# Result in two column tiles of 224 and 288 with one copy each, and the softmax sums by one matmul of two columns

One Trainium2 chip, one core. The metric is device time in microseconds of one execution; medians are of all runs of a kernel.

## The reference, cut to what matters

One decode step: layer norm, attention over the last 2048 of 8192 cached positions (8 sequences, 32 query heads, 8 key/value heads of 128), output projection, then an MLP (B's token shift is zero for one token).

```python
h  = x + attention(layernorm(x)) @ wo            # softmax(q k^T / sqrt(128)) v
y  = layernorm(h)                                # B's input
x1 = y                                           # the shifted branch is zero for S == 1
h2 = gelu(layernorm(x1) @ w3) @ w4               # w3 [512,1792], w4 [1792,512]
out = h + x1 + h2                                # [8, 1, 512] bf16
```

## The kernel before

PE is the matmul engine (TensorE) and PEld its weight loads, ACT is ScalarE, DVE is VectorE, SP is SyncE, which issues nearly all loads here, 79 MB. A loop over the 8 sequences transposes K on PE, makes scores, exponentials and the product with V. PSUM is the memory that the matmuls write. After the loop comes a tail: output projection, statistics, product with w3 (L729), gelu into `gT`, product with w4 (L757), copies out of PSUM, store. Parts that the change and the argument touch (cuts marked `...`):

```python
W4_CUT = [0, 8, 12, 13, 14]        # chunks of 128 rows of w4 in each of four loads
...
def pe_LB(e):                      # softmax sums of two halves, summed in PSUM
    for half in range(2):
        ins = e.matmul(LB, lspread..., lsum[:, half:half + 1], start=(half == 0), stop=(half == 1))
    ins.then_inc(sem_LB, 1)
def dve_rL(e, b):
    e.wait_ge(sem_LB, b + 2)
    e.reciprocal(rL[:, :], LB).then_inc(dve_self, 1)
...
NQ = 4; DQ = D // NQ               # four column strips of 128
fin_ps = b6[:, 0:DQ]
def pe_fin(e):
    ...                            # the residual (hi and lo halves) into PSUM, L749
    e.wait_ge(sem_actP, ACTP_G)    # gT is there
    for fc in range(FC):           # 14 chunks of w4
        if fc in W4_CUT:
            e.wait_ge(sem_w4[W4_CUT.index(fc)], 16)
        for j in range(NQ):        # L757: strip j, written to PSUM partitions 32j..
            ins = e.matmul(fin_ps[32 * j:32 * j + B, :], gT[:, fc * B:(fc + 1) * B],
                           w4_sb[:, fc, j * DQ:(j + 1) * DQ], start=False, stop=(fc == FC - 1),
                           tile_position=(0, 32 * j), ...)
            if fc == FC - 1:
                ins.then_inc(sem_peP, 1)
def dve_final(e):                  # strips 0 and 2; act_final does 1 and 3
    for j in range(0, NQ, 2):
        e.wait_ge(sem_peP, PEP_FIN[j])
        ins = e.tensor_copy(out_sb[:, j * DQ:(j + 1) * DQ], fin_ps[32 * j:32 * j + B, :])
    ins.then_inc(sem_dveP, 1)
```

The product has 8 columns of weights, the batch (128\*8 in the profile), and the kernel sets strip j at `tile_position=(0, 32 * j)`. The strips of a chunk run beside each other: the last chunk's four matmuls, of 263 ns or more each, start from 188.74 on and are all done 0.28 us later.

## Time and profile before

| | before |
|---|---|
| time, median (range) of the first 3 runs | 193.14 us (193.06 to 193.16) |
| span of the profiled execution | 191.4 us |
| busy: PE, ACT, DVE | 76%, 49%, 45% |
| HBM read over the span | 414 GB/s (428 to 435 in most slices) |
| first w4 chunk used / last chunk used | 186.90 / 188.74 us |
| store issued | 189.72 us |

The time is that of the loads, plus a tail of 2.7 us from the last landing (188.7) to the end of the span. A change here shortens the time only if it shortens this tail, and lengthens it if it lengthens the tail or makes some engine fall behind the loads. The lines of the profile are in the prediction.

### The profile page before, as it was taken

The numbers are of one execution on the slowest core, as the hardware profiler recorded it, in microseconds if no ns is written. First come the engines' busy times: TensorE is split into PE (matmuls) and PEld (weight loads), VectorE is DVE, ScalarE is ACT, GpSimd is POOL, SyncE is SP. The second block draws the span as 40 slices with busy tenths as digits, with TensorE's granted clock in tenths as the row PEclk, the third lists the DMA queues.
The fourth block names the chain that finished last, engine by engine and source line by source line (L and its number), as shares of the span: only waits on it lengthen the run. The fifth ranks groups of instructions, "written<-read, shape, count | busy, mean of one in ns | idle before, by whom it ended". The sixth has DMA issues, their size and how long they took to land. (4 is left out here: it accounts for less than half of the span.)

```text
span 191.4 us, 6341 instructions
## 1 busy us (share of the span) xinstructions
PE 145.6 (76%) x2848; PEld 116.9 (61%) x2848; DVE 85.8 (45%) x183; ACT 94.2 (49%) x119; POOL 6.4 (3%) x17
## 2 busy tenths in 40 slices
PE   2038996499878975998589849985998599886754
PEld 0014964487676754876577639764976577676642
DVE  7922656145625560457055604571446254640031
ACT  3031772657277724671678147725672586253041
POOL 8400000000000000000000000000000000000000
PEclk9999999669999999799999987999699999999655
DMA  6999999999999999999999999999999999999991
GB/s 228 431 435 428 421 419 443 428 428 431 428 435 426 435 431 426 431 431 431 435 428 435 435 424 431 431 431 435 428 435 435 424 431 431 431 435 411 412 400 43
DMA packets 6473, 79.31 MB, mean 414 GB/s; under 512 B 688, under 2 KB 960, under 8 KB 1856
## 3 DMA queue, kind: packets, MB, share of 16 engines
q1 hardware_dynamic: 6448, 79.18, 97.3%
q8 instruction: 6, 0.10, 0.2%
q14 instruction: 3, 0.02, 0.0%
q10 hardware_dynamic: 16, 0.01, 0.0%
HBM read 79.18 MB, written 0.01 MB: 414 GB/s over the span
## 5 line engine op out<-in xcount | busy, mean ns | idle before, releaser
L436 PE MATMUL kT_ps<-perm_b,slots 128*128 128x128 bf16 x1024 | 74.4, 235 | 15.2 <-PEq L421 15.2
L458 ACT ACTIVATE kT_sb<-kT_ps 128x1024 bf16<-128x1024 bf16 x64 | 65.1, 1023 | 36.6 <-PE kT_ps L436 36.4
L436 PEld LDWEIGHTS kT_ps<-perm_b,slots 128*128 128x128 bf16 x1024 | 66.0, 106 | 25.8 <-issue 25.8
L462 DVE COPY kT_sb<-kT_ps 128x1024 bf16<-128x1024 bf16 x64 | 44.3, 692 | 65.5 <-PE kT_ps L436 65.5
L501 ACT ACTIVATE P_sb<-S_ps,mtile 128x1024 bf16<-128x1024 f32 x16 | 17.7, 1108 | 31.3 <-DVE mtile L496 31.3
L476 PE MATMUL S_ps<-kT_sb,qcur 128*32 128x512 bf16 x256 | 25.7, 392 | 0.0
L533 PE MATMUL misc<-slots,pT_sb 128*32 128x128 bf16 x1024 | 16.2, 220 | 5.9 <-PEq L421 5.9
L533 PEld LDWEIGHTS misc<-slots,pT_sb 128*32 128x32 bf16 x1024 | 14.8, 97 | 8.2 <-issue 7.7
L523 DVE TENSOR_TENSOR pT_sb<-kT_ps,mask 128x1024 bf16<-128x1024 bf16 x18 | 12.4, 691 | 7.9 <-PE kT_ps L452 7.9
L452 PE MATMUL kT_ps<-perm_p,P_sb 128*128 128x128 bf16 x144 | 11.0, 221 | 0.0
L552 PE MATMUL b<-o_sum,selw 128*128 128x32 f32 x56 | 7.4, 276 | 4.3 <-PEq L421 4.3
L452 PEld LDWEIGHTS kT_ps<-perm_p,P_sb 128*128 128x128 bf16 x144 | 8.2, 98 | 3.6 <-issue 3.6
L476 PEld LDWEIGHTS S_ps<-kT_sb,qcur 128*32 128x32 bf16 x256 | 6.6, 93 | 6.0 <-issue 0.2
L552 PEld LDWEIGHTS b<-o_sum,selw 128*128 128x128 f32 x56 | 6.8, 191 | 5.3 <-issue 5.3
L542 DVE TENSOR_SCALAR o_sum<-misc,rL 128x128 f32<-128x128 f32 x8 | 2.8, 351 | 8.1 <-PE misc L533 8.1
L286 DVE TENSOR_SCALAR ident_f<-iota_f 128x128 f32<-128x128 f32 x1 | 5.7, 5682 | 1.3 <-POOL iota_f L207 1.3
L344 PE MATMUL b<-ident_b,xln_b 8*128 8x8 bf16 x4 | 0.3, 174 | 7.5 <-DVE xln_b L320 7.5
L287 DVE TENSOR_SCALAR ident_b<-iota_f 128x128 bf16<-128x128 f32 x1 | 5.6, 5606 | 0.0
L485 DVE TENSOR_REDUCE mtile<-S_ps 128x1 f32<-128x512 f32 x8 | 5.4, 673 | 0.0
L344 PEld LDWEIGHTS b<-ident_b,xln_b 8*128 8x128 bf16 x4 | 0.2, 113 | 8.3 <-DVE xln_b L320 8.3
L664 PE MATMUL S_ps<-opl,slots 128*128 128x8 bf16 x128 | 3.7, 168 | 1.8 <-issue 1.6
L508 PE MATMUL S_ps<-lsum,lspread 128*128 128x1 f32 x36 | 5.0, 244 | 0.0
(91 smaller groups left out, 66.2 us busy)
## 6 DMA issues: line engine op xcount, KB each, us to landing
slots<-in_A_k_cache_dram SPq DMA_DIRECT2D x16, 2048.0 KB, 13.5
slots<-in_A_v_cache_dram SPq DMA_DIRECT2D x16, 2048.0 KB, 17.0
slots<-in_A_wq_dram SPq DMA_DIRECT2D x1, 4096.0 KB, 12.1
slots<-in_A_wo_dram SPq DMA_DIRECT2D x2, 1024.0 KB, 21.5
slots<-in_A_wo_dram SPq DMA_DIRECT2D x1, 2048.0 KB, 26.0
slots<-in_B_w_dram SPq DMA_DIRECT2D x2, 896.0 KB, 30.7
slots<-in_B_w_dram SPq DMA_DIRECT2D x1, 1024.0 KB, 29.4
slots<-in_B_w_dram SPq DMA_DIRECT2D x1, 512.0 KB, 28.3
```

The costliest lines, as they stand in the source:

```text
L286: e.tensor_single_scalar(ident_f[:], iota_f[:], 0.0, ALU.is_equal)
L287: ins = e.tensor_single_scalar(ident_b[:], iota_f[:], 0.0, ALU.is_equal)
L436: ins = e.matmul(kT_ps[t % 2][:, c * 128:(c + 1) * 128], src[:, c * 128:(c + 1) * 128], perm_b[:, :], is_transpose=True)
L452: ins = e.matmul(kT_ps[half][:, c * 128:(c + 1) * 128], P_sb[:, k * 128:(k + 1) * 128], perm_p[:, :], is_transpose=True)
L458: e.activation(kT_sb[:, i % NKT, 0:W // 2], kT_ps[i % 2][:, 0:W // 2], ACT.Copy).then_inc(sem_Elo, 1)
L462: e.tensor_copy(kT_sb[:, i % NKT, W // 2:W], kT_ps[i % 2][:, W // 2:W]).then_inc(sem_Ehi, 1)
L476: ins = e.matmul(S_ps[32 * gl:32 * (gl + 1), 0, :], qcur[:, GL * gq + gl, o:o + 32], kv[:, gl, :, :], start=(t == 0), stop=(t == 2 * NT - ...
L485: ins = e.tensor_reduce(mtile[:, 1, 0:1], S_ps[:, 0, :], AX.X, ALU.max)
L501: e.activation(P_sb[:, half * W // 2:(half + 1) * W // 2].rearrange("r (k g) -> r k g", g=GL), bass.AP(tensor=S_ps[:, :, :].tensor, offset ...
L523: e.tensor_tensor(bass.AP(tensor=pT_sb[:, :, :, :].tensor, offset=h0 * NT * 48, ap=[[CT * NT * 48, 128], [48, CT // 2 * NT], [32, 2], [1, ...
L533: ins = e.matmul(pv_ps[32 * q:32 * (q + 1), :], pT_sb[:, c, q, 16 * gq:16 * gq + 32], slots[:, slot, k * DH:(k + 1) * DH], start=(gq == 0 ...
L552: ins = e.matmul(op_ps(b), selw[:, q, :], o_sum[:, NJ * q:NJ * (q + 1)], start=(q == 0), stop=(q == 3))
```

## The change

Its intent: fewer and larger instructions at the end. Two strips of 224 and 288 columns give 28 matmuls in place of 56 and one copy on each of DVE and ACT in place of two; SP waits for one semaphore. The two sums of the softmax come from one two-column matmul, and DVE adds them. The diff, cut to its core:

```diff
-        NQ = 4
-        DQ = D // NQ
+        N_CUT = [0, 224, 512]
+        NQ = 2
+        DQ = D // KC
...
-        LB = S_ps[:, 1, 0:1]
+        LB = S_ps[:, 1, 0:2]
...
-                for half in range(2):
-                    ins = e.matmul(LB, lspread..., lsum[:, half:half + 1], start=(half == 0), stop=(half == 1))
-                ins.then_inc(sem_LB, 1)
+                e.matmul(LB, lspread..., lsum[:, :], start=True, stop=True).then_inc(sem_LB, 1)
...
-            e.reciprocal(rL[:, :], LB).then_inc(dve_self, 1)
+            ins = e.tensor_reduce(lhs[:, :], LB, AX.X, ALU.add)
+            chain(e, ins, "dve_self", dve_self)
+            e.reciprocal(rL[:, :], lhs[:, :]).then_inc(dve_self, 1)
...
-        fin_ps = b6[:, 0:DQ]
+        fin_at = lambda j: b6[32 * j:32 * j + B, 0:N_CUT[j + 1] - N_CUT[j]]
...                              (the residual: ten matmuls, cut at the strips' and blocks' edges)
-                    ins = e.matmul(fin_ps[32 * j:32 * j + B, :], gT[:, fc * B:(fc + 1) * B],
-                                   w4_sb[:, fc, j * DQ:(j + 1) * DQ], ...
+                    ins = e.matmul(fin_at(j), gT[:, fc * B:(fc + 1) * B],
+                                   w4_sb[:, fc, N_CUT[j]:N_CUT[j + 1]], ...
...
+        def out_tile(e, j, copy):
+            e.wait_ge(sem_peP, PEP_FIN[j])
+            copy(out_sb[:, N_CUT[j]:N_CUT[j + 1]], fin_at(j)).then_inc(sem_done, 1)
+
+        DV.append(lambda e: out_tile(e, 0, e.tensor_copy))
+        AC.append(lambda e: out_tile(e, 1, lambda o, i: e.activation(o, i, ACT.Copy)))
```

More of the change, by code (lines that the diff above doesn't have):

```diff
@@ L106, in bass_sequential_preLN__sliding_block_cached__mixer_s_mlp__decode_kernel @@
         rL = sb([128, 1], dt.float32, "rL")
+        lhs = sb([128, 1], dt.float32, "lhs")
         iota_f = sb([128, 128], dt.float32, "iota_f")
@@ L148, in bass_sequential_preLN__sliding_block_cached__mixer_s_mlp__decode_kernel @@
         sem_out = S("sem_out")
+        sem_done = S("sem_done")
         act_self = S("act_self")
@@ L267, in sp_prog @@
                                     ).then_inc(sem_w4[i], 16)
-            e.wait_ge(sem_dveP, DVEP_OUT_READY)
-            e.wait_ge(sem_actP, ACTP_OUT_READY)
+            e.wait_ge(sem_done, NQ)
             e.dma_start(out.rearrange("b s d -> (b s) d"), out_sb[:, :]).then_inc(sem_out, 16)
@@ L506, in pe_LB @@
             if e is not None:
-                for half in range(2):
-                    ins = e.matmul(LB, lspread[:, :, :].rearrange("p q h -> p (q h)"), lsum[:, half:half + 1],
-                                   start=(half == 0), stop=(half == 1))
-                ins.then_inc(sem_LB, 1)
+                e.matmul(LB, lspread[:, :, :].rearrange("p q h -> p (q h)"), lsum[:, :], start=True, stop=True).then_inc(sem_LB, 1)
         def dve_rL(e, b):
             e.wait_ge(sem_LB, b + 2)
-            e.reciprocal(rL[:, :], LB).then_inc(dve_self, 1)
+            ins = e.tensor_reduce(lhs[:, :], LB, AX.X, ALU.add)
+            chain(e, ins, "dve_self", dve_self)
+            e.reciprocal(rL[:, :], lhs[:, :]).then_inc(dve_self, 1)
             cnt["dve_self"] += 1
@@ L747, in pe_fin @@
             for half in (hpx_hi, hpx_lo):
-                for k in range(KC):
-                    e.matmul(fin_ps[32 * k:32 * k + B, :], half[:, k * B:(k + 1) * B], ident_b[:, :],
-                             start=(half is hpx_hi), stop=False, tile_position=(0, 32 * k), skip_group_check=True)
+                for j in range(NQ):
+                    for k in range(KC):
+                        n0, n1 = max(N_CUT[j], k * DQ), min(N_CUT[j + 1], (k + 1) * DQ)
+                        if n0 < n1:
+                            e.matmul(fin_at(j)[:, n0 - N_CUT[j]:n1 - N_CUT[j]], half[:, k * B:(k + 1) * B],
+                                     ident_b[:, n0 - k * DQ:n1 - k * DQ],
+                                     start=(half is hpx_hi and n0 == N_CUT[j]), stop=False,
+                                     tile_position=(0, 32 * j), skip_group_check=True)
             e.wait_ge(sem_actP, ACTP_G)
@@ L756, in pe_fin @@
                 for j in range(NQ):
-                    ins = e.matmul(fin_ps[32 * j:32 * j + B, :], gT[:, fc * B:(fc + 1) * B],
-                                   w4_sb[:, fc, j * DQ:(j + 1) * DQ], start=False, stop=(fc == FC - 1),
+                    ins = e.matmul(fin_at(j), gT[:, fc * B:(fc + 1) * B],
+                                   w4_sb[:, fc, N_CUT[j]:N_CUT[j + 1]], start=False, stop=(fc == FC - 1),
                                    tile_position=(0, 32 * j), skip_group_check=True)
@@ L762, in bass_sequential_preLN__sliding_block_cached__mixer_s_mlp__decode_kernel @@
         PE.append(pe_fin)
-        DVEP_OUT_READY = ev_dve.next()
-        def dve_final(e):
-            for j in range(0, NQ, 2):
-                e.wait_ge(sem_peP, PEP_FIN[j])
-                ins = e.tensor_copy(out_sb[:, j * DQ:(j + 1) * DQ], fin_ps[32 * j:32 * j + B, :])
-            ins.then_inc(sem_dveP, 1)
-        DV.append(dve_final)
-        ACTP_OUT_READY = ev_act.next()
-        def act_final(e):
-            for j in range(1, NQ, 2):
-                e.wait_ge(sem_peP, PEP_FIN[j])
-                ins = e.activation(out_sb[:, j * DQ:(j + 1) * DQ], fin_ps[32 * j:32 * j + B, :], ACT.Copy)
-            ins.then_inc(sem_actP, 1)
-        AC.append(act_final)
+        def out_tile(e, j, copy):
[3 more added lines that the diff above has]
+        AC.append(lambda e: out_tile(e, 1, lambda o, i: e.activation(o, i, ACT.Copy)))
         with nc.Block() as block:
```

## The prediction

> **What bounds the kernel now.** I read, in this order: the page, the chain that ended last, the DMA issues, the order in time of the last 4.6 us, and the busy time and granted clock in stretches of it. Section 2 of the page first.
>
> ```profile
> DMA  6999999999999999999999999999999999999991
> GB/s 228 431 435 428 421 419 443 428 428 431 428 435 426 435 431 426 431 431 431 435 428 435 435 424 431 431 431 435 428 435 435 424 431 431 431 435 411 412 400 43
> ...
> by line: DMA slots<-in_B_w_dram 14.8%; PE kT_ps L436 0.6%; PE b L757 0.6%; SPq L265 0.2%; ACTq L782 0.1%; ACT xln_b L778 0.1%; issue 0.1%
> ...
> 159.74 28.26 DMA slots<-in_B_w_dram
> 187.99 0.04 issue
> 188.04 1.06 PE b L757 x23
> 189.09 0.26 ACT xln_b L778
> 189.35 0.28 ACTq L782
> ```
>
> From the second slice to the last but one, the DMA engines are full (DMA digit 9) at some 430 GB/s, and 79.31 MB have to come in. No compute engine is near its limit: PE is busy 76%, ACT 49%, DVE 45%. The chain says the same: it rests on a load of w4 that lands at 187.99, and only then turns to compute: 1.06 us of the last product, two copies on ACT. What follows the landing is the one stretch where an engine's speed is the kernel's speed. This is that stretch, as the timeline gives it (start, duration, engine, line, operation, count).
>
> ```profile
> 186.87 0.77 PEld L757 LDWEIGHTS b<-slots,gT 128*8 128x8 bf16 x32 [1.05 <-ACT gT L740]
> 186.90 2.12 PE L757 MATMUL b<-slots,gT 128*8 128x128 bf16 x56 [0.80 <-DMA slots<-in_B_w_dram]
> 188.04 0.46 PEld L757 LDWEIGHTS b<-slots,gT 128*8 128x8 bf16 x20 [0.40 <-DMA slots<-in_B_w_dram]
> 188.74 0.09 PEld L757 LDWEIGHTS b<-slots,gT 128*8 128x8 bf16 x4 [0.25 <-DMA slots<-in_B_w_dram]
> 189.05 0.58 DVE L769 CAST xln_b<-b 8x128 bf16<-8x128 f32 x2 [4.29 <-PE b L757]
> 189.08 0.55 ACT L778 ACTIVATE xln_b<-b 8x128 bf16<-8x128 f32 x2 [3.00 <-PE b L757]
> 189.72 0.37 SPq L270 DMA_DIRECT2D out_dram<-xln_b  x1
> ```
>
> PE follows the loads: chunks 0 to 7 of w4 (32 weight loads, four a chunk) begin at 186.87, as the first w4 load lands; 8 to 12 at 188.04; 13 at 188.74. Between the bursts PE stands idle for w4. So PE keeps up with the loads, and after the last one there is a single chunk (0.28 us) to do. The clock matters as well; the columns are us, busy and number on PE, PEclk, DMA share, GB/s.
>
> ```profile
> 13.01 1.02 PE L367 MATMUL S_ps<-slots,xlnT 128*8 128x512 bf16 x7 [1.76 <-DMA slots<-in_A_wq_dram]
> 13.81 1.07 PE L367 MATMUL S_ps<-slots,xlnT 128*8 128x512 bf16 x8
> 14.24 1.07 PE L367 MATMUL S_ps<-slots,xlnT 128*8 128x512 bf16 x8
> 14.67 1.07 PE L367 MATMUL S_ps<-slots,xlnT 128*8 128x512 bf16 x8
> ...
> 178.38:181.79 3.41, 2.90 (x102) 0.50 1.03 420
> 181.79:185.21 3.42, 1.91 (x45) 0.50 1.01 410
> 185.21:188.62 3.41, 2.50 (x78) 0.50 0.57 217
> ```
>
> From 178.38 to the end PE is granted half of its clock. The L367 lines come from a stage of the same build (four column strips, 8 columns of weights, but 512 columns moved): its groups of four start 427 ns apart (13.81, 14.24, 14.67). Narrow windows on L757 show groups of four starting at 187.07, 187.18, 187.28, 187.40, 187.50, 187.60: 107 ns apart for 128 columns. Both are columns / 1.2 per ns for four matmuls at once. So the strips run beside each other, and a round of them costs the columns of its widest strip.
>
> [...] here a small reciprocal takes 203 ns from SBUF (L699) and 157 from PSUM (L514).
>
> **The change, part by part.**
>
> *Softmax sums.* One f32 matmul with two moving columns replaces two with one each: the trace has 4 PE entries per batch at L508, 250 ns each, started some 140 ns apart; two go, about 0.28 us of PE a batch. DVE gets a two-column reduce out of PSUM (about 0.16 to 0.21 us, from the 157 ns of the reciprocal there and the 208 ns of the small reduce L489), a wait for itself, and the reciprocal now reads SBUF (0.20 for 0.16). That is about 0.3 us more per batch. In the loop neither counts, since the DMA queue is full. In the last batch the reciprocal ends at 172.17 and its user waits for PE until 173.88: the added 0.3 us fits in the gap of 1.7. PE's 0.28 us earlier only makes the chain earlier that makes gT, and gT is ready at 186.08, 0.79 us before w4. Worth 0.
>
> *Residual into PSUM (L749).* Eight matmuls of 128 columns become ten of 32 to 128; from 185.71 at half clock, at most about 0.7 us, done before 186.87. Worth 0.
>
> *The last product (L757).* Four strips of 128 columns become two of 224 and 288. This removes half of the instructions, but also half of what runs beside each other. A chunk now takes 288 / 1.2 = 240 ns for 107. With 14 chunks: 14 x 240 = 3.36 us for 1.49. PE no longer keeps up with w4: chunk 8 could start at 186.90 + 8 x 0.24 = 188.82, after the load for it (188.0) and even the last load (188.74) have landed. So the waits for w4 disappear from the second on, and PE itself sets the end. A first matmul with 128 columns takes 263 ns, with 288 thus 263 + 160/1.2 = 396. The end of the wide strip is 186.90 + 13 x 0.24 + 0.396 = 190.42; before, it was 189.02. Cost: 1.40 us.
>
> *The copies.* Before, two per engine: 0.58 us on DVE, 0.55 on ACT. After, one each. ACT's slope is from 128 columns (269 ns, L778) to 512 (597 ns, L377): 0.854 ns a column, so 288 columns take 269 + 137 = 406 ns. DVE: 282 ns for 128, 692 for 512 (L384), so 224 columns take 385 ns, and its strip ends earlier. ACT ends at 190.42 + 0.04 + 0.41 = 190.87; before, both were done at 189.63. Gain in the copies 0.15 us. One wait of SP less is worth about 0.02 (the semaphore instruction there takes 17 ns).
>
> Sum: +1.40 - 0.15 - 0.02 = +1.23 us; the store would be issued at 190.95 for 189.72. 193.14 + 1.23 = 194.37; I take 0.05 off for the chance of a faster clock, below: 194.3.
>
> **The rivals.**
>
> *The loads still set the end.* Then only the copies' gain would stay: 193.0 us. For it speaks that the chain rests on w4. It needs a chunk in 120 ns, which is the full clock. [...] Against it: a window with PE busy 2.90 of 3.41 us (178.38 to 181.79) did not raise the clock[...]. [...] I give it one in eight.
>
> *The two strips do not overlap well.* With strictly one after the other a chunk takes (224 + 288) / 1.2 = 427 ns, 14 take 5.97 us: 2.6 us more, 196.9. The steps of L367 and L757 speak against it, as four strips overlap fully there.
>
> *The sums become a wait.* If the longer DVE path held up the next maximum and with it the loop, each batch could cost 0.3 us, 2.4 us in all. Against it: the DMA share is about 1.0 in every stretch from 15 to 185 us, so the loads have work queued throughout; and DVE waits 65.5 us in the loop for the transposes (L462). I expect 0.
>
> **Range and chances.** The step of 240 ns is the term that counts, and it comes from two measured steps at the same clock. Below the estimate lies the faster clock[...]; above it, [...]scatter of 0.1. Range 193.8 to 194.6. 2% is 3.9 us; no rival alone gets there, and a gain is bounded by the tail after the loads.
>
> **What would show it.** In the changed kernel's trace: pairs at L757's place starting 240 ns apart without idle time for w4 after the first chunk; its last matmul ending near 190.4; copies of about 0.385 and 0.41 us, once each; the store issued near 190.95; the chain that ended last with about 3.5 us of this product in place of 1.06; the same 430 GB/s to 185 us. I am wrong if PE still waits for w4 in bursts (the full clock, or a cost by something other than columns), if the steps are near 427 ns, or if the loop's GB/s fell.

The sum came to +1.40 - 0.15 - 0.02 = +1.23 us, or 194.37. The last step to 194.3, that is when and by what the clock rises and what a rise would gain, the 0.05 us taken off and the "one in eight" stand as the author's estimate. So does the upper end of the range, since a loss between strips that it allowed for was shown by no trace. What the trace of the kernel before shows of the clock is stretches of half clock of 6.82 us (from 35.02) and three times 3.42 us (from 75.97, 113.52 and 134.00), and half clock from 178.38 to the end.

## The result, and the profile after

| | before | after |
|---|---|---|
| time, median of 6 runs | 193.15 us (193.06 to 193.59) | 194.30 us (193.78 to 194.56) |
| ratio after / before, 95% interval | | 1.005 (1.0033 to 1.0068) |
| profiled execution: span | 191.4 us | 192.7 us |
| store issued in it | 189.72 us | 190.97 us |

A ratio is the mean time of one kernel's fast runs over that of the other's fast runs of the same rounds, so it is not quite the ratio of the medians. The verdict at 2% is "same"; the interval shows that the changed kernel is slower by about half a per cent.

In the changed kernel the page's line of data rates, and the last pieces of the chain that ended last (start, duration, what):

```profile
GB/s 226 435 422 435 429 413 447 422 429 432 429 430 432 435 432 420 435 435 429 435 432 425 432 432 432 435 429 432 432 425 435 435 429 435 425 432 406 415 337 5
```

```profile
185.34 1.97 PE misc L730 x56
187.31 0.58 PE b L753 x8
187.89 2.63 PE b L763 x25
190.52 0.02 issue
190.54 0.40 ACT xln_b L775
```

The loads run at the same rates, but the chain no longer goes back to one: it is PE work through L730, L753 and the product, now L763. The same stretch in order of time:

```profile
187.35 0.26 ACT L741 ACTIVATE gT<-misc 128x112 bf16<-128x112 f32 x1 [0.82 <-PE misc L730]
187.66 2.52 PEld L763 LDWEIGHTS b<-slots,gT 128*8 128x8 bf16 x28
187.67 2.84 PE L763 MATMUL b<-slots,gT 128*8 128x224 bf16 x28
190.43 0.38 DVE L772 CAST xln_b<-b 8x224 bf16<-8x224 f32 x1 [4.13 <-PE b L763]
190.54 0.40 ACT L775 ACTIVATE xln_b<-b 8x288 bf16<-8x288 f32 x1 [2.93 <-PE b L763]
190.97 0.37 SPq L272 DMA_DIRECT2D out_dram<-xln_b  x1
```

The product is one stretch without a wait for w4 (before: three bursts), it lasts 2.84 us, and the copies take 0.38 and 0.40 us, once each. The end at 190.97 is the predicted 190.95, yet by a way that was not predicted in two points. The product starts at 187.67 and not at 186.90, because `gT` is ready only at 187.61; and the clock rises inside it. The granted clock (PEclk, the share of full speed that PE is given) over L763, cut where it changes (us, busy and number on PE, then on PEld, PEclk, DMA share, GB/s):

```profile
187.70:189.60 1.90, 1.90 (x19) 1.66 (x21) 0.50 0.05 16
189.60:190.50 0.90, 0.90 (x12) 0.49 (x8) 1.00 0.00 0
```

At half clock throughout, a start at 187.67 and the predicted length of 3.52 us (13 x 0.24 + 0.396) would have ended at 191.19; it ended at 190.50. So 0.77 us of a late start and 0.69 us of a faster clock nearly cancel in this execution. One matching end time does not confirm the working; the experiments have to.

### The profile page after: what moved, and what is told of

It reads as the page before. It is cut to its first block, busy times and chain, and to the rows that moved or that the text cites. A ratio compares the mean times of both kernels' runs of the same rounds, so it can differ in the third digit from the quotient of the medians.

```text
span 192.7 us, 6258 instructions
## 1 busy us (share of the span) xinstructions
PE 146.3 (76%) x2804; PEld 117.9 (61%) x2804; DVE 86.8 (45%) x190; ACT 94.0 (49%) x118; POOL 6.4 (3%) x17
## 5 line engine op out<-in xcount | busy, mean ns | idle before, releaser
L438 PE MATMUL kT_ps<-perm_b,slots 128*128 128x128 bf16 x1024 | 76.2, 238 | 16.0 <-PEq L423 16.0
L438 PEld LDWEIGHTS kT_ps<-perm_b,slots 128*128 128x128 bf16 x1024 | 67.9, 108 | 26.5 <-issue 26.5
L369 PE MATMUL S_ps<-slots,xlnT 128*8 128x512 bf16 x32 | 3.6, 626 | 1.9 <-DMA slots<-in_A_wq_dram 1.9
```

What stands on the lines that cost most here:

```text
L438: ins = e.matmul(kT_ps[t % 2][:, c * 128:(c + 1) * 128], src[:, c * 128:(c + 1) * 128], perm_b[:, :], is_transpose=True)
```

## The experiments

Theory: a chunk of the product costs the columns of its widest strip over the granted clock (240 ns at half of it, and by halving an estimated 120 at full), PE rather than the last load sets the end, and when the clock falls and rises differs from execution to execution (the second table below). Rivals: the lost time comes from the sums, through a late PE chain; the pace follows the sum of the columns or the number of strips; the last load still sets the end. Eleven kernels ran, in three sets, each set on one chip with its own runs of the kernel before (medians 193.18, 193.08 and 193.15 us, 11 runs each, 192.92 to 194.02).

| kernel | median us (range), 6 runs | ratio to before (95%) |
|---|---|---|
| after_again | 194.19 (194.03 to 194.49) | 1.0046 (1.0027 to 1.0066) |
| fin_only | 194.46 (194.12 to 194.96) | 1.0064 (1.0043 to 1.0085) |
| lb_only | 193.17 (193.13 to 193.38) | 0.9996 (0.9977 to 1.0016) |
| two_copies | 194.46 (194.18 to 195.58) | 1.0068 (1.0041 to 1.0095) |
| cut_256_256 | 194.16 (193.70 to 195.00) | 1.0042 (1.0024 to 1.0060) |
| cut_128_384 | 195.20 (194.59 to 195.82) | 1.0103 (1.0082 to 1.0123) |
| fill_after | 195.23 (194.21 to 197.08) | 1.0116 (1.0077 to 1.0155) |
| fill_before | 194.13 (193.21 to 195.69) | 1.0059 (1.0026 to 1.0091) |
| strips4_copy1 | 193.36 (193.14 to 194.17) | 1.0014 (0.9996 to 1.0032) |
| early_w4_after | 194.22 (193.86 to 195.64) | 1.0077 (1.0047 to 1.0106) |
| early_w4_before | 193.22 (193.02 to 193.40) | 1.0004 (0.9992 to 1.0016) |

What each trace shows of the tail, read from its order of time and its granted clock. "Half clock" is how long the stretch of half clock lasted that lies near 152 us, in the last pass of the loop; "rise" is when the clock went up again at the end:

| trace | half clock near 152, us | gT ready | product from | product to | rise | store issued |
|---|---|---|---|---|---|---|
| before | none | 186.08 | 186.90 | 189.02 | none | 189.72 |
| lb_only | 3.4 | 185.98 | 186.81 | 188.92 | none | 189.62 |
| after | 6.8 | 187.61 | 187.67 | 190.50 | 189.60 | 190.97 |
| after_again | 3.4 | 186.52 | 186.58 | 190.16 | 190.83 | 190.63 |
| fin_only | 3.4 | 186.06 | 186.80 | 190.05 | 189.63 | 190.51 |
| two_copies | none | 185.96 | 186.78 | 190.31 | none | 190.82 |
| cut_256_256 | 6.8 | 187.81 | 187.86 | 191.02 | none | 191.49 |
| cut_128_384 | 3.4 | 186.02 | 186.84 | 190.60 | 189.54 | 191.14 |
| early_w4_after | 3.4 | 186.26 | 186.32 | 189.90 | 190.11 | 190.37 |

### The changed kernel once more: after_again (no edit)

> The changed kernel, unedited, for a second trace. Theory (the product is paced by its widest strip over the granted clock[...]): runs between 193.6 and 194.6 us; pairs of the last product 240 ns apart while the clock is at 0.5 and 120 ns apart where it is at 1.0; the instant of the rise, against the start of the product, differs from the first trace (189.55 with the product from 187.67). Rival (the lateness of the PE chain in the first trace, 187.67 for 186.90, is made by the change): the product starts again 0.8 us later than in the kernel before.

```profile
186.26 0.26 ACT L741 ACTIVATE gT<-misc 128x112 bf16<-128x112 f32 x1 [0.82 <-PE misc L730]
186.58 3.59 PE L763 MATMUL b<-slots,gT 128*8 128x224 bf16 x28
189.97 0.38 DVE L772 CAST xln_b<-b 8x224 bf16<-8x224 f32 x1 [4.76 <-PE b L763]
190.20 0.40 ACT L775 ACTIVATE xln_b<-b 8x288 bf16<-8x288 f32 x1 [3.68 <-PE b L763]
190.63 0.37 SPq L272 DMA_DIRECT2D out_dram<-xln_b  x1
```

Here `gT` is ready at 186.52, 0.09 us after the first w4 load has landed (186.44), and the clock stays at half to the product's end: the product takes 3.59 us for the predicted 3.52. It begins 0.32 us earlier than predicted, and the store goes out 0.32 us earlier, at 190.63 for 190.95. The late start of the first trace did not come back, so the change does not make it in every execution. Whether it makes it likelier, the traces cannot tell: `gT` comes after 187.6 in two of the eight with two strips, and in none of the five with four. What goes with it is seen in the granted clock of the last pass of the loop. First the changed kernel's first trace, then this one (us, busy and number on PE, PEclk, DMA share, GB/s):

```profile
152.10:155.50 3.40, 2.48 (x24) 0.50 1.01 434
155.50:158.80 3.30, 3.30 (x32) 0.50 1.00 427
```

```profile
152.10:155.50 3.40, 2.68 (x30) 0.67 1.01 434
155.50:158.80 3.30, 3.30 (x45) 0.82 1.00 427
```

In the first trace PE stood at half clock in both stretches and issued 56 matmuls in 6.7 us, here 75. In the table the two traces with 6.8 us of half clock there are the two with `gT` after 187.6; all others have it between 185.96 and 186.73 (early_w4_before). That is a correlation over 13 traces, not an experiment on the clock.

### The result part alone: fin_only

```diff
 (the changed kernel; lhs, LB, pe_LB and dve_rL as before)
```

> Only the result part of the change (two strips of 224 and 288, one copy each); the softmax sums as before. Theory: as the changed kernel, 194.3 us, +1.1 us against before, within 0.2. Rival (the sums part has a share in the loss): at least 0.3 us under the changed kernel of the same rounds.

194.46 us against 194.19 of the changed kernel on the same chip. Without the sums part the loss is all there, so the rival that gives the sums a share of it falls. The difference of 0.27 us has the wrong sign for it and lies within the scatter of either kernel.

### The sums part alone: lb_only

```diff
 (the kernel before, with LB, pe_LB and dve_rL of the change)
```

> Only the softmax sums part of the change; the result in four strips as before. Theory: 0 within 0.1 us of before, 193.15. Rival (the longer DVE path, two instructions for one in each of 8 batches, delays the loop or the PE chain): up to 0.3 us a batch, 2.4 us in all, or about 0.8 us through the PE chain at the end.

193.17 us, ratio 0.9996: worth nothing, as predicted. The DVE instructions in this trace (number, then minimum, median and maximum in ns):

```profile
L512 DVE TENSOR_REDUCE lhs<-S_ps x8: 148/150/151, 49.9 to 172.1; 128x1 f32<-128x2 f32 x8
L514 DVE RECIPROCAL rL<-lhs x8: 164/164/165, 50.1 to 172.3; 128x1 f32<-128x1 f32 x8
```

The path is longer by 150 ns, a short wait, and 7 ns of the reciprocal (157 before); the last one ends at 172.42, while its user waits for PE until 173.94.

### Where the strips are cut: cut_256_256 and cut_128_384

```diff
-        N_CUT = [0, 224, 512]
+        N_CUT = [0, 256, 512]        (cut_256_256)
+        N_CUT = [0, 128, 512]        (cut_128_384)
```

> The changed kernel with strips of 256 and 256 columns. Theory: the step is 256/1.2 = 213 ns for 240; the product is 13*0.027+0.027 = 0.37 us shorter at half clock: about 193.95 us when the clock does not rise, down to 193.4 when it does; median 193.9, 0.3 under the changed kernel. Rival (the cost is one of two strips in place of four, whatever their width, or of the sum of the columns): as the changed kernel, 194.3.

> The changed kernel with strips of 128 and 384 columns. Theory: the step is 384/1.2 = 320 ns; 195.5 us when the clock stays at 0.5, less when it rises within the product[...]: 194.2 to 195.5, median 194.9. Rival (the sum of the columns sets the pace, 512 in every cut): as the changed kernel, 194.3.

Three narrow windows of the trace of cut_128_384 each begin with the next wide matmul, at half clock; then the whole product of cut_256_256:

```profile
187.45 0.84 PE L763 MATMUL b<-slots,gT 128*8 128x384 bf16 x3
187.77 0.84 PE L763 MATMUL b<-slots,gT 128*8 128x384 bf16 x3
188.09 0.84 PE L763 MATMUL b<-slots,gT 128*8 128x384 bf16 x3
```

```profile
187.86 3.16 PE L763 MATMUL b<-slots,gT 128*8 128x256 bf16 x28
```

Steps of 320 ns are 384 / 1.2. The length of 3.16 us is 13 x 213 ns + 0.37 (0.263 + 128/1.2 ns) = 3.14. All cuts move 512 columns a chunk with two strips; the pace follows the widest strip, so both rivals about the pace fall. In the times cut_128_384 costs 1.0% where 0.9% was expected (its median of 194.9 counted on a rise within the product, an estimate; in the one trace it came at 189.54); cut_256_256 is not told apart from the changed kernel (194.16, expected 193.9): its traced execution is one with a late `gT` (195.0 us), and the scatter of 1.3 us is larger than the 0.3 us sought. It rests on its trace.

### The copies: two_copies

```diff
-            copy(out_sb[:, N_CUT[j]:N_CUT[j + 1]], fin_at(j)).then_inc(sem_done, 1)
+            n0, n1 = N_CUT[j], N_CUT[j + 1]
+            h = (n1 - n0) // 2
+            copy(out_sb[:, n0:n0 + h], fin_at(j)[:, 0:h])
+            copy(out_sb[:, n0 + h:n1], fin_at(j)[:, h:n1 - n0]).then_inc(sem_done, 1)
```

> The changed kernel with each strip copied by two instructions of half the columns (112+112 on DVE, 144+144 on ACT). Theory: the fixed cost of one more copy per engine comes back: DVE 282-16*1.07=265 ns twice = 0.53 for 0.385, ACT (269+16*0.854=283) twice = 0.57 for 0.41; +0.15 us against the changed kernel, seen in the trace, hard to see in the times. If the copies were of no account, 0.

```profile
186.78 3.53 PE L763 MATMUL b<-slots,gT 128*8 128x224 bf16 x28 [0.54 <-DMA slots<-in_B_w_dram]
190.11 0.26 DVE L774 CAST xln_b<-b 8x112 bf16<-8x112 f32 x1 [5.48 <-PE b L763]
190.34 0.45 ACT L778 ACTIVATE xln_b<-b 8x144 bf16<-8x144 f32 x2 [4.38 <-PE b L763]
190.82 0.37 SPq L272 DMA_DIRECT2D out_dram<-xln_b  x1
```

This execution began with the w4 load and stayed at half clock, exactly as the prediction had it: 3.53 us for 3.52. The second copy on ACT costs 0.05 us (0.45 for 0.40), not the 0.16 expected: ACT's two copies overlap by 0.09 us (190.34 to 190.63 and 190.53 to 190.80). In the kernel before they did not (189.08 to 189.35 and 189.36 to 189.63): there the second had a semaphore wait of its own ahead of it, here it has none. So part of what the second copy would add (0.09 us here) is hidden behind the first. From the product's end to the store's issue it is 0.51 us here, 0.47 in after_again and 0.70 in the kernel before (189.02 to 189.72). So 0.19 of the 0.23 us that the change gains behind the product are still there with two copies per engine. So they do not come from the number of copies; that they come from the semaphore waits that fell away (one between the copies of each engine, one on SP) is the author's reading, as no run takes a wait away alone. The times (194.46 and 194.19) cannot tell 0.05.

### More work for the clock: fill_after and fill_before

```diff
+        def pe_fill(e, n):
+            for _ in range(n):
+                e.matmul(kT_ps[1][:, 0:1024].bitcast(dt.float32), ident_b[:, :], kT_sb[:, 0, 0:512], start=True, stop=True)
+        PE.append(lambda e: pe_fill(e, 1))      (after the projection)
+        PE.append(lambda e: pe_fill(e, 3))      (after the statistics)
+            pe_fill(e, 3)                       (before the wait for gT in the last product)
```

> The changed kernel with seven matmuls of 512 columns that nobody reads, put where PE waits in the tail (1 after the projection, 3 after the statistics, 3 before the last product), to have the clock risen when the last product begins. Theory (columns over the clock): granted clock 1.0 in the product, steps of 120 ns, PE keeps up with the w4 loads again, end set by the last load: 193.0 to 193.2 us, equal to or up to 0.15 under the kernel before. Rival (the cost of two strips has nothing to do with the clock): 194.3 or more.

> The kernel before with the same seven idle matmuls. Theory: the last load sets the end in either clock; only the last chunk gets shorter: 193.05 to 193.15 us, same as before within 0.1.

That more matmuls would bring the full clock in time was the guess; the first trace of the changed kernel had shown a rise at 189.60 after PE had been busy 3.39 of 3.39 us (186.20 to 189.59). Both expectations failed: 195.23 and 194.13 us. In the traces the clock did not rise before the product (fill_after: 0.50 until 190.02), and the idle matmuls got in its way. (The one traced execution of fill_before, 193.21 us, is near the kernel before, but there the product waits for the idle matmuls until 187.33 and then runs in one stretch of 1.66 us, so that PE and not the last load sets its end.) Granted clock in fill_after (columns as above), and then two lines of its order of time:

```profile
183.20:186.60 3.40, 3.16 (x69) 0.50 1.02 404
186.61:190.02 3.41, 3.41 (x25) 0.50 0.16 61
190.04:190.90 0.86, 0.81 (x11) 1.00 0.00 0
```

```profile
186.59 1.46 PE L682 MATMUL kT_ps<-kT_sb,ident_b 128*128 128x512 bf16 x3
187.98 2.87 PE L771 MATMUL b<-slots,gT 128*8 128x224 bf16 x28
```

After the first stretch, in which PE was busy 3.16 of 3.40 us, mostly with the w3 product's 8-column matmuls, the clock stayed at half; after the next, 3.41 of 3.41 us with matmuls of 224 to 512 columns, it rose, at 190.03, too late. In that trace `gT` was ready at 186.37, and the product waited for the filler until 187.98. So the experiment does not test what the kernel would do at full clock. That the steps halve when the clock doubles is shown by the traces in which it rises inside the product: in the first of the changed kernel the wide matmuls start at 189.73, 189.85, 189.97, 190.10 and 190.22, 122 to 123 ns apart; in fill_after at 190.19, 190.31, 190.44 and 190.56. Why single runs of the filled kernels are up to 2.5 us longer than their traced ones stays open; only one execution of each is traced.

### When the product starts: early_w4_after and early_w4_before

```diff
-        W4_CUT = [0, 8, 12, 13, 14]
+        W4_CUT = [0, 4, 8, 12, 13, 14]          (and a fifth semaphore, and L719's index)
```

> The changed kernel with the first w4 load (chunks 0 to 7) cut in two of four chunks, so that the first chunks are there about 1 us earlier (512 KB at 430 GB/s are 1.2 us). Theory (in the changed kernel PE sets the end from the first chunk on, so that its start counts in full): the product starts when gT is ready, 0.05 us after it, instead of at the landing near 186.9; 0.1 to 0.6 us less than the changed kernel, about 193.9. Rival (the last load sets the end): no change, 194.3.

> The kernel before with the same cut of the first w4 load. Theory (the last load sets the end there): no change, within 0.1 us of before; the product starts earlier in the trace and waits longer for its later chunks.

Of early_w4_after:

```profile
186.00 0.26 ACT L741 ACTIVATE gT<-misc 128x112 bf16<-128x112 f32 x1 [0.83 <-PE misc L730]
186.32 3.59 PE L763 MATMUL b<-slots,gT 128*8 128x224 bf16 x28
190.37 0.37 SPq L272 DMA_DIRECT2D out_dram<-xln_b  x1
```

The first half of the load lands at 185.48 and the second at 186.72. The product starts with `gT` and not at a landing, and keeps its length of 3.59 us; the store goes out at 190.37, 0.26 earlier than in after_again, which started 0.26 later. In these two traces the start counts in full, as the theory says. In the times the expectation failed: the median, 194.22 for about 193.9, shows no gain, and two of the six runs took 195.43 and 195.64. Times of that size fit a late `gT` at half clock (an estimate from the traces: cut_256_256 took 195.0 that way, and 13 x 27 + 27 = 0.38 us more for 224/288 columns gives 195.4), but those runs were not traced. In early_w4_before nothing moves (1.0004): the last load sets the end there. Its traced product starts no earlier either, at 186.78, since `gT` came only at 186.73.

### One copy per engine with four strips: strips4_copy1

```diff
 (kernel before; o4 is [128, 128] bf16; the waits on PEP_FIN[1] and PEP_FIN[3] stay)
+            ins = e.tensor_copy(o4[0:32 + B, :], b6[0:32 + B, 0:DQ])
+            e.activation(o4[64:96 + B, :], b6[64:96 + B, 0:DQ], ACT.Copy).then_inc(sem_actP, 1)
+            for j in range(2):                  (on SP; ACT stores strips 2 and 3 likewise)
+                e.dma_start(out_j(j), o4[32 * j:32 * j + B, :]).then_inc(sem_out, 16)
```

> The kernel before (four strips of 128, sums as before) with one copy per engine by another way: DVE copies partitions 0 to 39 (strips 0 and 1) and ACT partitions 64 to 103 (strips 2 and 3) in one instruction each, and four small stores, two from SP and two from ACT, in place of one. Theory: the product stays at 107 ns a chunk and the copies go from 0.58 to 0.28 us, so a first store at about 189.4 for 189.72; what the second store of a queue adds (0.37 us is the duration of one issue) decides: -0.3 us if they overlap, +0.1 if they are issued one after the other. 192.85 to 193.25.

```profile
189.03 0.28 DVE L769 CAST o<-b 40x128 bf16<-40x128 f32 x1 [4.32 <-PE b L758]
189.10 0.27 ACT L777 ACTIVATE o<-b 40x128 bf16<-40x128 f32 x1 [3.07 <-PE b L758]
189.35 0.71 SPq L271 DMA_DIRECT2D out_dram<-o  x2
189.41 0.64 ACTq L780 DMA_DIRECT2D out_dram<-o  x2
```

The copies are halved, 0.28 for 0.58 us, with the product at four strips. The issues of two stores on one queue, one after the other (0.71 us), take it back: the second goes out at 189.76, where the single store before went out at 189.72. No gain: the median of 193.36 lies above the expected range (192.85 to 193.25), the ratio is 1.0014. A form with a single store was not run.

## Why the prediction was right, point by point

The time, 194.3, is the measured median, and the mechanism is the one named: the product no longer follows the loads, PE sets the end.

- **Step of 240 ns.** Confirmed where the clock stays at half: 3.59 us (after_again) and 3.53 (two_copies) for 3.52; and by the other cuts, 320 and 213 ns. Only the picture of pairs was wrong: in after_again the wide strip's matmuls start 240 ns apart, but the narrow strip's 187 ns (224 / 1.2), and these run up to four chunks ahead. The wide strip alone sets the pace. The copy of the narrow strip gains nothing by that lead: its last matmul (chunk 13) starts at 188.96, before the wide strip's of chunk 10 (189.00), and its records end at 189.35 (matmul ends are modelled in the profile), but DVE's copy of it starts only at 189.97, 0.05 us after the end of the wide matmul of chunk 12 (189.92).
- **The second step it rests on (L367).** The prediction takes that stage as half clock without saying that the profile prints a PEclk of 1.00 there. The trace holds no clock record before 21.36 us, so this 1.00 is no reading. That the clock was half is borne out by the loop's transposes (L436, 128 columns): they start 107 ns apart up to 21.3 us and 56 ns apart from 21.4 us on, while the printed PEclk is 1.00 on both sides. From 17.95 us to that change of pace PE did only transposes (L393, L436).
- **Start with the first w4 load.** Right in fin_only, two_copies and cut_128_384 (186.78 to 186.84). In the first trace of the changed kernel it failed: `gT` came at 187.61. The prediction took the 0.79 us between `gT` and w4 in one trace for a margin; the traces show it to vary from 0.8 us in hand (two_copies) to 0.9 short (after and cut_256_256, where `gT` is ready 0.94 and 0.87 us after the first w4 load has landed). In the changed kernel all of a late start counts (0.26 us in the start and 0.26 in the store, early_w4_after against after_again), since no wait for w4 is left to absorb any of it.
- **Clock.** "One in eight" for a rise inside the product was too low: of the five traces with the 224/288 product and no filler it rose before the product's end in two (after, fin_only). The stretch cited against it (PE busy 2.90 of 3.41 us) held mostly 8-column matmuls. So did the one in fill_after that left the clock at half (3.16 of 3.40 us). With mostly the product in it, 2.94 of 3.40 us was followed by a rise in fin_only (at 189.63), and 2.73 of 3.40 us in after_again (at 190.83); but 3.41 of 3.41 us in cut_256_256 was not (186.14 to 189.55, of which the product had the last 1.7 us). What decides the granted clock is not shown. The 0.05 us taken off for it was too little by itself (the rise in the first trace gained 0.69 us, and one eighth of that would already be 0.09); the late starts, not foreseen, go the other way. That the centre of 194.3 was hit so well owes something to this.
- **Copies.** 0.38 and 0.40 us for 0.385 and 0.406. The gain behind the product was a little larger than predicted, 0.23 us (after_again) for 0.17, and the reason given, the fixed cost of a second copy, is the smaller part of it: two_copies pays 0.04 us for the second copies. The DVE copy starts only 0.23 us before ACT's in after_again, so the 224 columns gain nothing on the path, as predicted.
- **Sums, residual.** 0, as predicted. The parts of the sums were over-estimated: the reduce takes 150 ns for 160 to 210, and the reciprocal from SBUF 164 for 203, a figure that was read off an 8-column one. The residual took 0.65 us for "at most about 0.7".
- **Rivals.** "The loads still set the end" and "the strips do not overlap" are excluded by the traces, "the sums become a wait" by lb_only. What two strips would cost with the full clock from the product's start was not reached by any run.

## What to carry to other kernels

In this kernel a product in column strips cost its widest strip: half the instructions, in strips 2.25 times as wide, took 240 ns a chunk for 107, and PE had half clock from 179.4 us on, to the end in the kernel before and to 189.60 in the first trace of the changed one. Before merging strips, compare the new pace with the pace of the loads: the last of 14 chunks landed 1.84 us after the first load (186.90 to 188.74), which leaves 142 ns for each of the 13 before it; 107 ns a chunk kept up with that, 240 ns did not, and 1.4 us were lost in the product to save 0.23 behind it. Where one trace ends on time, look whether it got there by the steps predicted, for a late start and a faster clock may cancel.
